# Tokens loaded in runs of two with block-diagonal K and V, a staged head and loads issued from ScalarE, in a windowed-attention and maxout feed-forward kernel

## Chip, cores and metric

One core of a Trainium2 chip. The metric is the device time of one execution in microseconds (us), median of several. A run whose time is over 1.5% above the fastest run of the same kernel is called slow; verdicts use fast runs alone, with a 95% interval, and 2% is the threshold for "faster" or "slower". Engines: TensorE (PE, its weight loads PEld), VectorE (DVE), ScalarE (ACT), GpSimd (POOL) and SyncE (SP). A "q" behind an engine's name in a profile line means its instruction stream issuing a DMA.

## The reference

Attention over 4 batches, 8 heads, 768 tokens and 64 columns per head, with a causal window of 128 and 4 sink tokens; its output, 3072 tokens of 512, goes through a three-way maxout and one more matrix.

```python
scores = scale * np.matmul(q, k.transpose(0, 1, 3, 2))
rel = pos[:, None] - pos[None, :]
keep = (pos[None, :] < n_sink) | ((rel >= 0) & (rel < window))
a = softmax(np.where(keep, scores, -1e9))          # written out in the original
x = (a @ v).transpose(0, 2, 1, 3).reshape(B * S, H * D)
h = np.maximum(np.maximum(x @ w1, x @ w2), x @ w3)  # 512 -> 768
return (h @ w_out).astype(np.float32)               # 768 -> 512
```

## The kernel before

The work is cut into 12 chunks of 256 tokens (3 per batch). For each chunk: load K, Q, V in float32 (SyncE), cast to bf16 (GpSimd), transpose K and Q (TensorE), scores, exp (ScalarE), mask (DVE), attention times V (called AV below, with a 65th column of ones that gives the softmax sum), transpose of the result, then nine groups of feed-forward matmuls (h) and two output tiles (y). The feed-forward of one chunk is interleaved with the attention of the next.

```python
def load(ci):                      # one partition per token: 256-byte runs
    for n in range(2):             # t0: the first token of half n
        for j, src in ((0, k), (1, q)):
            nc.sync.dma_start(out=qk[:, n, j], in_=src[b, :, t0:t0 + 128].rearrange("h p d -> p h d"))
    for n in range(2):
        nc.sync.dma_start(out=vr[:, n], in_=v[b, :, t0:t0 + 128].rearrange("h p d -> p h d"))

load(0)
# ... identity and masks (GpSimd) ...
for i in range(2):                 # zeros on DVE: half of each K pair is zero
    nc.vector.memset(kz[i][64:128, :, 0, :], 0.0)
    nc.vector.memset(kz[i][0:64, :, 1, :], 0.0)
    nc.vector.memset(ve[i][:, :, :, D:D + 1], 1.0)
    # ... zeros of ks ...
# ... nine weight tiles and wo, all issued by GpSimd here ...
load(1)
# ... sink rows vs_raw (SyncE), their products on GpSimd ...

def av(ci, qd, t):                 # one head per matmul: 65 columns
    # ... sink matmul ...
    for hh in range(4):
        p, h = divmod(4 * qd + hh, 2)
        # blocks: the one or two key blocks in the window
        for i, (sl, kb) in enumerate(blocks):
            nc.tensor.matmul(o[:, hh], lhsT=es[ci, p][:, h, sl], rhs=ve[b % 2][:, kb, 2 * p + h, :], ...)

cast(0, True)                      # chunk 0 on DVE and ACT
# prep(0), cast(1), load(2), all scores, AV and transposes of chunk 0,
# prep(1), cast(2), load(3), and only then the first feed-forward matmul
```

The softmax here doesn't subtract the row's maximum and nothing guards it: scores larger than these inputs give would overflow.

## Time and profile before

| | before |
|---|---|
| time, median of 3 runs | 237.43 us (236.39 to 238.04) |
| span in the profile, granted TensorE clock | 236.0 us, 1.000 |
| first score / first feed-forward matmul / first y matmul | 20.34 / 47.18 / 60.72 us |
| last matmul | 232.0 us |
| DMA packets | 84,070, of them 75,600 under 512 B |

A timeline line reads: start, duration, engine, source line, operation, output<-input, shapes, count; in brackets how long the engine had been idle and what ended it. A group line ends with busy time and mean ns, then the idle time before the group. The lines that carry the argument are in the prediction; one more is needed for comparison, the AV group:

```profile
L230 PE MATMUL o_ps<-ve,e_sb 128*128 128x65 bf16 x352 | 19.8, 197 | 5.8 <-DVE e_sb L202 4.4
```

There are 352 matmuls of 65 columns, and TensorE waited 5.8 us in all ahead of them.

### The profile page before, as it was taken

Reading aid. Unit: us, or ns where it says so; the run is one execution under the profiler, and the core shown is the slowest. Engines: PE = TensorE matmul, PEld = TensorE weight load, DVE = VectorE, ACT = ScalarE, POOL = GpSimd, SP = SyncE. Lnnn points to the kernel's source line nnn. Section 1 sums busy time; section 2 is a strip of 40 time slices with the busy share of each in tenths; the row PEclk is TensorE's granted clock in tenths of the full one; section 3 lists DMA queues with packets and bytes.
Section 4 is the critical chain, followed back from the end, with each engine's and each line's share of the span. In section 5 each row is a group of like instructions: output and inputs, shape, how many; then the busy total and the mean of one; then the engine's idle time right before and its main releaser. Section 6 shows DMA issues by size and latency. Waiting matters only on the chain.

```text
span 236.0 us, 4886 instructions
## 1 busy us (share of the span) xinstructions
PE 190.7 (81%) x1968; PEld 153.7 (65%) x1968; DVE 134.1 (57%) x307; ACT 112.9 (48%) x215; POOL 55.1 (23%) x79
## 2 busy tenths in 40 slices
PE   0025600499998999999979999999899999999993
PEld 0013400389687786887967887968768879789681
DVE  6841500247577397395685773964857739547350
ACT  2016300146465545664744547556545475574411
POOL 8840005953015005032060140330500400000000
PEclk9999999999999999999999999999999999999999
DMA  7999988990196194591881964916919720020202
GB/s 150 194 184 183 191 167 158 174 205 3 47 213 102 55 213 92 164 187 51 184 136 46 205 109 132 204 23 175 185 47 200 114 89 3 1 92 0 92 0 89
DMA packets 84070, 28.65 MB, mean 121 GB/s; under 512 B 75600, under 2 KB 80976, under 8 KB 84048
## 3 DMA queue, kind: packets, MB, share of 16 engines
q1 hardware_dynamic: 78496, 25.20, 51.0%
q0 software_dynamic: 5552, 3.15, 9.3%
q8 instruction: 15, 0.25, 0.5%
q14 instruction: 7, 0.06, 0.1%
HBM read 25.20 MB, written 6.29 MB: 133 GB/s over the span
## 4 chain that ended last, share of the span: by engine, by line
PE 57%; DVE 17%; SPq 11%; ACT 5%; DMA 4%; issue 3%; POOL 2%; POOLq 0%; ACTq 0%; DVEq 0%
PE h_ps L260 29%; PE y_ps L271 10%; SPq L64 8%; DVE h_sb L266 5%; DVE e_sb L202 5%; PE o_ps L230 4%; PE pt L163 4%; SPq L68 3%; DVE kz L170 3%; DMA v_raw<-in_v_dram 3%; PE st L191 3%; ACT e_sb L199 2%; PE xt_ps L249 2%; DVE x_sb L238 2%; ACT h_sb L264 2%
## 5 line engine op out<-in xcount | busy, mean ns | idle before, releaser
L260 PE MATMUL h_ps<-xT,w 128*128 128x256 bf16 x864 | 109.9, 274 | 0.0
L260 PEld LDWEIGHTS <-w 128*128 128x128 bf16 x864 | 81.3, 98 | 9.0
L199 ACT ACTIVATE e_sb<-st 128x512 bf16<-128x512 f32 (+1 forms) x96 | 53.8, 564 | 36.9 <-PE st L193 36.9
L202 DVE TENSOR_TENSOR e_sb<-e_sb,msk 128x1024 bf16<-128x1024 bf16 (+1 forms) x48 | 33.6, 699 | 64.4 <-ACT e_sb L199 63.9
L266 DVE TENSOR_TENSOR h_sb<-h_sb,h_ps 128x512 bf16<-128x512 bf16 x72 | 49.3, 684 | 9.6 <-PE h_ps L260 7.5
L148 POOL CAST qk_bf<-qk_raw 128x1024 bf16<-128x1024 f32 x22 | 23.8, 1086 | 103.3 <-DMA qk_raw<-in_q_dram 103.3
L163 PE MATMUL pt<-ident,qk_bf 128*128 128x128 bf16 x192 | 20.0, 236 | 33.1 <-POOL qk_bf L148 14.8
L163 PEld LDWEIGHTS <-qk_bf 128*128 128x128 bf16 x192 | 13.8, 105 | 35.1 <-POOL qk_bf L148 15.3
L271 PE MATMUL y_ps<-wo,h_sb 128*128 128x512 bf16 x144 | 35.2, 380 | 0.0
L274 ACT COPY y_sb<-y_ps 128x512 f32<-128x512 f32 x24 | 14.0, 585 | 37.1 <-PE y_ps L271 37.1
L170 DVE COPY kz<-pt 64x512 bf16<-64x512 bf16 x48 | 20.1, 418 | 17.5 <-PE pt L163 16.9
L191 PE MATMUL st<-qT,kz 128*128 128x256 bf16 x96 | 27.2, 284 | 1.9 <-ACT qT L166 1.2
L264 ACT CAST h_sb<-h_ps 128x512 bf16<-128x512 f32 x36 | 21.1, 585 | 9.9 <-PE h_ps L260 9.1
L230 PE MATMUL o_ps<-ve,e_sb 128*128 128x65 bf16 x352 | 19.8, 197 | 5.8 <-DVE e_sb L202 4.4
L230 PEld LDWEIGHTS <-e_sb 128*128 128x128 bf16 x352 | 17.2, 100 | 8.1 <-DVE e_sb L202 5.2
L166 ACT COPY qT<-pt 128x512 bf16<-128x512 bf16 x24 | 14.1, 586 | 17.0 <-PE pt L163 17.0
L193 PE MATMUL st<-qT,kz 128*128 128x128 bf16 x96 | 22.0, 229 | 0.0
L238 DVE TENSOR_TENSOR x_sb<-o_ps,rc 128x256 bf16<-128x256 f32 x48 | 20.4, 425 | 1.7
L271 PEld LDWEIGHTS <-h_sb 128*128 128x128 bf16 x144 | 12.6, 98 | 12.2 <-DVE h_sb L266 1.9
L154 POOL CAST ve<-v_raw 128x512 bf16<-128x512 f32 x22 | 14.8, 681 | 3.5 <-DMA v_raw<-in_v_dram 2.6
L250 ACT COPY xT<-xt_ps 128x512 bf16<-128x512 bf16 x24 | 13.1, 598 | 3.3 <-PE xt_ps L249 3.3
L189 PE MATMUL st<-qT,kz 128*128 128x128 bf16 x64 | 14.2, 222 | 0.0
(38 smaller groups left out, 104.6 us busy)
## 6 DMA issues: line engine op xcount, KB each, us to landing
qk_raw<-in_k_dram SPq DMA_DIRECT2D x24, 256.0 KB
qk_raw<-in_q_dram SPq DMA_DIRECT2D x24, 256.0 KB
v_raw<-in_v_dram SPq DMA_DIRECT2D x24, 256.0 KB
out_dram<-y_sb SPq DMA_DIRECT2D x24, 256.0 KB
w<-in_moe_w_dram POOLq DMA_DIRECT2D x9, 256.0 KB, 12.5
wo<-in_moe_w_out_dram POOLq DMA_DIRECT2D x2, 384.0 KB, 17.5
vs_raw<-in_v_dram SPq DMA_DIRECT2D x8, 4.0 KB
```

The lines of the kernel that those rows point to most:

```text
L148: nc.gpsimd.tensor_copy(qkb[:, n], qk[:, n].rearrange("p j h d -> p j (h d)"))
L163: nc.tensor.transpose(pt[:, p], qkb[:, n, j, p * 128:(p + 1) * 128], ident)
L170: nc.vector.tensor_copy(kz[b % 2][r, :, h, t0:t0 + 128], pt[r])
L191: nc.tensor.matmul(st[:, 1:3], lhsT=kzh[:, q0:q0 + 128], rhs=qh[:, q0:q0 + 256], start=True, stop=True)
L199: nc.scalar.activation(e[:, h, lo:], st[:, lo:], AF.Exp, scale=scale)
L202: nc.vector.tensor_mul(e[:, :, lo:], e[:, :, lo:], m)
L230: nc.tensor.matmul(o[:, hh], lhsT=es[ci, p][:, h, sl], rhs=ve[b % 2][:, kb, 2 * p + h, :], start=(c == 0 and i == 0), stop=(i == len(block ...
L238: nc.vector.tensor_mul(xs[ci, t][:, 4 * qd:4 * qd + 4], o[:, :, 0:D], rc.unsqueeze(2).to_broadcast([128, 4, D]))
L260: nc.tensor.matmul(hp[:, f], lhsT=w_sb[fp, wi][:, ds, f * 128:(f + 1) * 128], rhs=xTs[ci][:, ds, :], start=(ds == 0), stop=(ds == DS - 1))
L264: nc.scalar.copy(dst, hp)
L266: nc.vector.tensor_max(dst, dst, hp)
L271: nc.tensor.matmul(yp, lhsT=hs[ci][:, fb, t * 128:(t + 1) * 128], rhs=wo[:, fb], start=(fb == 0), stop=(fb == FB - 1))
```

## The change

It has two parts. **Layout:** a partition takes two adjacent tokens, so that a K or Q run is 512 bytes; K blocks and V blocks become block-diagonal over a pair of heads, the masks follow, and AV streams 130 columns. **Schedule:** the head of the program is staged: the sink rows come first, two groups of the loads are issued from ScalarE's stream at chosen points (so that they stay behind the arriving weights), the feed-forward of chunk 0 starts before chunk 1 is transposed, and zeros of the second batch move to GpSimd at a later point.

```diff
-        def load(ci):
-            qk = raw.tile([128, 2, 2, H, D], F32, ...)
-                    nc.sync.dma_start(out=qk[:, n, j], in_=src[b, :, t0:t0 + 128].rearrange("h p d -> p h d"))
+        def load(ci, eng):
+            qk = raw.tile([128, 2, H, 2, D], F32, ...)
+            vr = raw.tile([128, 2, NP, 2, D], F32, ...)
+            for g in range(2):
+                for j, src in ((0, k), (1, q)):
+                    eng.dma_start(out=qk[:, j, 4 * g:4 * g + 4],
+                        in_=src[b, 4 * g:4 * g + 4, t0:t0 + 256].rearrange("h (p i) d -> p h (i d)", i=2))
+            for h in range(2):
+                for n in range(2):
+                    eng.dma_start(out=vr[64 * h:64 * h + 64, n],
+                        in_=v[b, h::2, t0 + 128 * n:t0 + 128 * n + 128].rearrange("a (r i) d -> r a (i d)", i=2))
 ...
+        def zeros(i, eng):
+            eng.memset(kb_sb[i][64:128, :, :, :, :, 0:64], 0.0)
+            eng.memset(kb_sb[i][0:64, :, :, :, :, 64:128], 0.0)
+            eng.memset(vb_sb[i], 0.0)
 ...
+        zeros(0, nc.vector)
 ...
+        def sink_v_init():
 ...
+            nc.gpsimd.memset(vs, 0.0)
 ...
-                    nc.tensor.matmul(o[:, hh], lhsT=es[ci, p][:, h, sl],
-                                     rhs=ve[b % 2][:, kb, 2 * p + h, :],
+                    nc.tensor.matmul(o[:, 2 * a:2 * a + 2], lhsT=es[ci, p][:, i, sl],
+                                     rhs=vb_sb[b % 2][:, n // 2, n % 2, p, i],
 ...
+        for g in range(2):
             for j in range(2):
-                prep(0, n, j)
+                cast_qk(0, j, g, nc.vector)
+                prep(0, j, g)
+        cast_v(0)
+        run("Sa0 Sa1 Sa2", a=0)
+        load(1, nc.scalar)
+        run("Sa3 Sa4 Aa00 Sa5 Aa01 Sa6 Sa7", a=0)
+        sink_v_init()
+        sink_v(0)
         cast(1)
 ...
+        run("Fa0 Fa1 Kb0 Fa2 Qb0 Kb1 Qb1 Zb Sb0 Sb1 Sb2", a=0, b=1)
+        load(2, nc.scalar)
+        load_wo()
+        run("Fa3 Sb3 Sb4 Ab00 Fa4 Sb5 Ab01 Sb6 Fa5 Sb7 Ab10 Ab11 Tb0 Tb1", a=0, b=1)
         cast(2)
-        load(3)
+        load(3, nc.sync)
 ...
+        zeros(1, nc.gpsimd)
```

(S is a score, A an AV group, T a transpose of the result, F a feed-forward group, K and Q transposes, Z the sink scores; a and b are the chunks.)

## The prediction

> **What bounds the kernel now.** I read the page's slices first, then the groups by form, then the timeline of the head and of one steady chunk, then the chain.
>
> Slices (40 of 5.9 us each: TensorE, then DMA share):
>
> ```profile
> PE   0025600499998999999979999999899999999993
> DMA  7999988990196194591881964916919720020202
> ```
>
> TensorE is nearly empty for eight slices (47 us) while the DMA engines are full; from there on it is full to the end, and DMA has room. So there are two regimes with different limits.
>
> The head, from the timeline and the chain:
>
> ```profile
> 9.41 4.40 SPq L64 DMA_DIRECT2D qk_raw<-in_q_dram  x1
> 20.34 0.37 PE L191 MATMUL st<-qT,kz 128*128 128x256 bf16 x1 [0.67 <-ACT qT L166]
> 32.78 3.27 SPq L120 DMA_DIRECT2D vs_raw<-in_v_dram  x8
> 43.51 0.77 PEld L163 LDWEIGHTS <-qk_bf 128*128 128x128 bf16 x8 [15.05 <-POOL qk_bf L148]
> 47.18 1.92 PE L260 MATMUL h_ps<-xT,w 128*128 128x256 bf16 x8
> ```
>
> Chunk 1's loads are pushed into the SP queue while all weights stream; each issue takes 3 to 5 us. The sink rows come behind them at 32.78, and GpSimd, in order, will not cast chunk 1 before it has used the sink rows. So the first feed-forward matmul is at 47.18, although chunk 0's attention was finished at 29.35 (28.77 + 0.58, its last xT copy).
>
> The steady part: pieces of the chain, and one attention-times-V group of the timeline.
>
> ```profile
> 138.44 1.75 PE h_ps L260 x16
> 158.77 1.31 PE y_ps L271 x6
> ...
> 125.33 0.41 PE L230 MATMUL o_ps<-ve,e_sb 128*128 128x65 bf16 x8
> 125.55 0.10 PEld L220 LDWEIGHTS <-e_sink 128*128 128x128 bf16 x1
> 125.57 0.27 PE L220 MATMUL o_ps<-vs,e_sink 128*128 128x260 bf16 x1
> ```
>
> A 256-column matmul takes 1.75/16 = 109 ns, a 512-column one 1.31/6 = 218 ns, and eight 65-column AV matmuls run from 125.33 to 125.57, 30 ns each. From the starts of all matmuls in the trace I summed these costs: 178 us of necessary TensorE time; the first matmul is at 11.3 and the last at 232.0, so 43 us is idle or cold, 33 of it before the first y matmul at 60.7. The later iterations lose 0.2 to 2.0 us each, mostly before AV (DVE's mask). TensorE is **the** bound after 47 us; whatever is added to it there is paid.
>
> **What the Trainium skill says.** (1) "TensorE: Matmul & The Clock Gate", Back-to-back issue gap: warm gap is N/2.4 + 2.5 ns, which is 56 at 128, 109 at 256 and 216 at 512; the trace has 56, 109 and 216 (medians of starts). At 65 the trace has 30. (2) "DMA: Bandwidth & Descriptors", Queues, rings and completion order: each DMA engine alternates between the queues packet by packet. The packet records agree: from 10 to 24 us the SP queue moves about 490 packets of 256 B and the GpSimd queue about 494 of 512 B in each 2 us (61 and 123 GB/s), whereas the SP queue alone had 224 GB/s from 2 to 6 us. (3) The same page, Specifications: transfers need at least 512 B for line rate. No run yet shows 512 B reads here; 256 B packets took 22 ns and 2 KB packets 89 ns, so doubling the run to 512 B should cost far less than double (an estimate: 30 ns). (4) "VectorE: DVE Perf Modes", Zero memsets can be issued as uint32: a memset pays per element, whatever the type. The trace: 128x2080 bf16 in 1.79 us, 64x1536 uint32 in 1.34, both 0.87 ns per element.
>
> **The change, part by part.**
>
> *Runs of two.* A partition now holds two adjacent tokens, so Q/K/V packets are 512 B and half as many: 36,900 instead of 73,700. In the steady part DMA was not the limit (GpSimd's cast waits, 103 us in total, hold nobody up there), so this is worth nothing after 47 us. In the head it is: load 0 has 3,072 packets; at 30 ns on 16 engines about 6 us, so it lands near 9 us. Before, its last part was cast at 17.92 us.
>
> *Block-diagonal K.* Scores keep their number and columns: 8 x (128+256+128). Transposes, exps, masks and DVE copies keep count and size too (the instruction order shows 3,938 TensorE rows on both sides). Zero.
>
> *Block-diagonal V.* AV keeps 352 matmuls, but each streams both heads' columns, 130 instead of 65. By the formula that the other sizes obey, 130/2.4 + 2.5 = 57 ns instead of 30: 352 x 27 = **+9.5 us** of TensorE, all but 24 of the matmuls in or near the full part. I let 1 us of it be absorbed by waits for DVE: +8.5.
>
> *GpSimd and DVE.* Casts per chunk go from 2 x 1.09 + 2 x 0.68 = 3.5 us to about 4 x 0.65 + 2 x 1.1 = 4.8 us, out of 16: hidden. DVE's zeros at the start: 2 x 1.34 + 6,240 x 0.87 ns = 5.4 + small ones, ending near 10.6 us, as before (10.7). So earlier data doesn't start DVE's first cast earlier. The second batch's zeros go to GpSimd, some 13 us at its 1.02 ns per element (512 in 0.52 us); they lie between the casts of chunks 2 and 3, and TensorE needs the latter near 67 us, about when they are done: 0 to 2 us.
>
> *The staged head.* A walk with durations from the trace. DVE casts, K copies and sink copies in a chain with transposes: 10.6 to about 16.6, first score there (20.34 before, because ACT's qT copy stood behind the V cast, now on GpSimd). Exps at 0.53 us each; after the third, ACT issues load 1's eight DMAs. One issue took SP 0.41 us even for 4 KB (3.27/8), so **ACT is held 3.3 us at least**, up to 5 if the queue fills behind the weights. Remaining exps, AV, transposes: about 5.8 us. First feed-forward matmul at 18.2 + 4.1 + 0.5 + 5.8 = 28.6, against 47.18. Three of its groups and chunk 1's transposes and scores take to about 37.5; then load 2's issues hold ACT again for 3.3 to 4 us, of which TensorE has work for 1.5. Chunk 1's attention with groups 3 to 5 then takes 6 us, so TensorE is full from about 47.5. By then 15.1 us of its work are done, so 32.4 us are lost; 1.5 more for the less regular schedule of chunk 2: **34**.
>
> Sum: before, start and loss up to 60.7 were 44.0 (11.3 + 32.7); now 34. Work 178 becomes 187.5. Later losses were 10.0; with one iteration fewer and the absorbed microsecond, 7.5. Last matmul at 34 + 187.5 + 7.5 = 229, against 232.0. Last copy, store and end as before, 4 us: span 233, and the measured time was 1.4 above the span: 234.4.
>
> **The rivals.**
> (a) *The ACT issues are cheap or fall beside other work.* For it: they are a deliberate gate, so that load 1 stays behind the weights. Against: 0.41 us per issue on SP. It would give back up to 5 us: 229.
> (b) *The head collapses further*, since TensorE gets warm earlier and load 1 lands early: 226. Against: DVE's memsets fix the start at 10.6, and scores to xT took 9 us before.
> (c) *DMA back-pressure.* Load 1 alternates with 1 KB weight packets (96 ns each before), ACT is held for more than 5 us, twice. For it: SP's 3 to 5 us per issue before. It gives 237 to 239.
> (d) *AV's added columns hide.* They would if weight loads set the 30 ns, but the rule gives 57 ns for the stream itself, above any of them. I give it little; it would mean 226.
>
> **Range and chances.** The sum says 234.4. I lean to (a) a little, since gate and order look tuned on the chip, and put the time at 232, range 226 to 237.5. The 2% line is 232.7, just above: faster 0.54, within 2% 0.44, slower 0.02.
>
> **What will show it.** Starts of AV matmuls 57 ns apart, and AV's busy time up accordingly; 512 B packets at about 30 ns, 3,072 per load; DVE's first cast near 10.6; a gap of 3 to 5 us between the third and fourth exp of chunk 0, with ACT's DMA issues in it, and another in chunk 1; the first feed-forward matmul at 27 to 30; the PE row at 9 from the eighth or ninth slice. The prediction fails if AV is not 57 ns, if ACT's issues cost much less or more than 3.3 us, or if chunk 3's late zeros or a slower GpSimd cast open a new hole between 55 and 75 us.

## The result and the profile after

The changed kernel takes **250.68 us** (median of four fast runs, 250.38 to 252.25) against 237.74 (236.39 to 238.24). The ratio is 1.0567, 95% interval 1.0503 to 1.0631: slower. (A ratio here is the mean time of one kernel's fast runs over that of the other's in the same rounds, so not quite the ratio of the medians.) The result is correct.

From the starts of all matmuls I made the same sum as in the prediction. "Lost" is time in which TensorE had no matmul to do or ran one at a lower rate. (Twelve of the 144 y records are missing in the later traces; 12 x 0.216 us is put back as work.)

| us | before | predicted | after |
|---|---|---|---|
| start and time lost up to the first y matmul | 44.0 | 34 | **47.0** |
| needed TensorE work | 178 | 187.5 | 187.5 |
| lost later | 10.0 | 7.5 | 10.3 |
| last matmul | 232.0 | 229 | 244.7 |

The work is what was predicted. The head, which should have gained 10 us, lost 3. The slices of the page (6.2 us each) show where: TensorE's share rises early, then there is a hole in the eighth slice, and the clock dips in and behind it.

```profile
PE   0024487067999698999989999999899999999994
PEclk9999999758999999999999999999999999999999
DMA  6998996710001986183490671914806720020102
```

The timeline of the first half of the head:

```profile
5.48 5.26 DVE L93 MEMSET vb<- 128x6240 bf16 x1 [1.25 <-issue]
...
11.68 0.47 DVE L161 CAST qk_bf<-qk_raw 128x512 bf16<-128x512 f32 x1
...
13.68 1.82 POOL L146 MEMSET vs<- 128x2080 bf16 x1
13.76 1.80 DVE L202 COPY ks<-kb 128x4 bf16<-128x4 bf16 x4
...
20.93 0.43 ACTq L66 DMA_DIRECT2D qk_raw<-in_k_dram  x1
...
23.07 2.68 ACTq L71 DMA_DIRECT2D v_raw<-in_v_dram  x4
...
25.80 0.87 ACT L226 ACTIVATE e_sb<-st 128x384 bf16<-128x384 f32 x2 [4.39 <-DMA qk_raw<-in_k_dram]
...
26.93 0.40 PE L257 MATMUL o_ps<-vb,e_sb 128*128 128x130 bf16 x2 [4.78 <-DVE e_sb L228]
...
34.09 3.19 PE L288 MATMUL h_ps<-xT,w 128*128 128x256 bf16 x16 [0.67 <-ACT xT L277]
```

DVE clears V until 10.74 and casts first at 11.68. Four tiny copies take 1.80 us while GpSimd clears `vs`. ScalarE issues load 1 from 20.93 to 25.75 and starts no exp in that time; AV waits 4.78 us for it. The first feed-forward matmul is at 34.09, 13 us earlier than before. Its 16 matmuls take 3.19 us, against 16 x 0.109 = 1.75 at full rate.

The second hold:

```profile
43.97 0.52 ACTq L66 DMA_DIRECT2D qk_raw<-in_q_dram  x1
45.48 4.54 ACTq L71 DMA_DIRECT2D v_raw<-in_v_dram  x4
45.55 0.60 POOL L161 CAST qk_bf<-qk_raw 128x512 bf16<-128x512 f32 x1 [12.38 <-DMA qk_raw<-in_k_dram]
46.34 0.61 POOL L161 CAST qk_bf<-qk_raw 128x512 bf16<-128x512 f32 x1 [0.18 <-DMA qk_raw<-in_q_dram]
48.17 0.61 POOL L161 CAST qk_bf<-qk_raw 128x512 bf16<-128x512 f32 x1 [1.22 <-DMA qk_raw<-in_k_dram]
49.44 0.61 POOL L161 CAST qk_bf<-qk_raw 128x512 bf16<-128x512 f32 x1 [0.66 <-DMA qk_raw<-in_q_dram]
50.05 0.58 ACT L292 CAST h_sb<-h_ps 128x512 bf16<-128x512 f32 x1 [7.09 <-POOL qk_bf L161]
...
52.07 0.62 PE L257 MATMUL o_ps<-vb,e_sb 128*128 128x130 bf16 x4 [8.08 <-DVE e_sb L228]
52.48 1.91 PE L288 MATMUL h_ps<-xT,w 128*128 128x256 bf16 x8
...
61.29 6.28 PE L288 MATMUL h_ps<-xT,w 128*128 128x256 bf16 x56
```

ScalarE's next work comes at 50.05; since 42.43 (the start of its first issue of load 2) it had only issued DMAs: 7.6 us. Narrower windows give the starts of the four V issues: 45.48, 46.3, 48.14 and 49.41. GpSimd's casts, which wait for the K and Q transfers of the same load, start at 45.55, 46.34, 48.17 and 49.44. The semaphore records have these four transfers landed at 45.40, 46.29, 48.12 and 49.39. So each V issue went out at the moment when one K or Q transfer of its own load had landed. AV then waited 8.08 us; the eight matmuls behind it took 1.91 us, where eight later ones take 1.04, and TensorE is dense from 61.29, not from the predicted 47.5.

The AV group, and two lines of the steady part:

```profile
L257 PE MATMUL o_ps<-vb,e_sb 128*128 128x130 bf16 x352 | 31.4, 230 | 19.2 <-DVE e_sb L228 19.0
```

```profile
76.37 0.62 PE L257 MATMUL o_ps<-vb,e_sb 128*128 128x130 bf16 x8
76.83 0.22 PE L216 MATMUL st<-qT,kb 128*128 128x128 bf16 x1
```

Eight AV matmuls occupy 76.37 to 76.83, 57 ns each, as predicted; the waits in front of the group grew from 5.8 to 19.2 us, which are the two holes.

### The profile page after: what moved, and what is told of

It reads as the page before. It is cut to its first block, busy times and chain, and to the rows that moved or that the text cites. A ratio compares the mean times of both kernels' runs of the same rounds, so it can differ in the third digit from the quotient of the medians.

```text
span 248.7 us, 4928 instructions
## 1 busy us (share of the span) xinstructions
PE 202.2 (81%) x1956; PEld 164.4 (66%) x1968; DVE 139.5 (56%) x306; ACT 115.1 (46%) x213; POOL 84.7 (34%) x109
## 2 busy tenths in 40 slices
DMA packets 46006, 28.66 MB, mean 115 GB/s; under 512 B 2208, under 2 KB 42912, under 8 KB 45984
## 4 chain that ended last, share of the span: by engine, by line
PE 60%; DVE 21%; ACT 8%; issue 5%; ACTq 2%; DMA 2%; POOL 0%; DVEq 0%
PE h_ps L288 28%; PE y_ps L299 11%; PE o_ps L257 8%; DVE e_sb L228 5%; ACT e_sb L226 5%; DVE kb L194 4%; DVE h_sb L294 4%; PE pt L186 4%; PE st L218 3%; DMA qk_raw<-in_q_dram 2%; DVE vb L93 2%; PE xt_ps L276 2%; DVE ks L202 2%; ACT qT L189 2%; DVE x_sb L265 2%
## 5 line engine op out<-in xcount | busy, mean ns | idle before, releaser
L288 PEld LDWEIGHTS <-w 128*128 128x128 bf16 x864 | 82.5, 99 | 10.9 <-issue 1.0
L161 POOL CAST qk_bf<-qk_raw 128x512 bf16<-128x512 f32 x44 | 27.8, 636 | 106.4 <-DMA qk_raw<-in_k_dram 86.4
L257 PE MATMUL o_ps<-vb,e_sb 128*128 128x130 bf16 x352 | 31.4, 230 | 19.2 <-DVE e_sb L228 19.0
L257 PEld LDWEIGHTS <-e_sb 128*128 128x128 bf16 x352 | 25.1, 102 | 23.2 <-DVE e_sb L228 21.9
L299 PE MATMUL y_ps<-wo,h_sb 128*128 128x512 bf16 x132 | 32.7, 379 | 0.6
L170 POOL CAST vb<-v_raw 64x1024 bf16<-64x1024 f32 x24 | 27.0, 1125 | 6.2 <-DMA v_raw<-in_v_dram 5.3
L218 PE MATMUL st<-qT,kb 128*128 128x256 bf16 x96 | 27.1, 286 | 0.7 <-ACT e_sb L226 0.7
L189 ACT COPY qT<-pt 128x512 bf16<-128x512 bf16 x24 | 17.5, 735 | 20.8 <-PE pt L186 20.8
L220 PE MATMUL st<-qT,kb 128*128 128x128 bf16 x96 | 22.0, 229 | 0.0
L194 DVE COPY kb<-pt 64x512 bf16<-64x512 bf16 x48 | 20.1, 419 | 3.0 <-PE pt L186 2.5
L277 ACT COPY xT<-xt_ps 128x512 bf16<-128x512 bf16 x24 | 13.2, 595 | 8.5 <-PE xt_ps L276 8.5
L216 PE MATMUL st<-qT,kb 128*128 128x128 bf16 x64 | 14.2, 221 | 0.4 <-ACT e_sink L238 0.3
```

The costliest lines, as they stand in the source:

```text
L161: eng.tensor_copy(bfs[ci][:, j, g].rearrange("p i (h d) -> p h i d", d=D), qk[:, j, 4 * g:4 * g + 4])
L170: nc.gpsimd.tensor_copy(vb_sb[b % 2][hp, c, :, :, :, h, 0:D].rearrange("p n a i d -> p (n a i) d"), vr[hp].rearrange("p n a i d -> p (n a ...
L194: nc.vector.tensor_copy(kb[hp, c, :, 2 * g:2 * g + 2, :, 64 * h:64 * h + 64] .rearrange("p i a n r -> p i (a n) r"), pt[hp].rearrange("p i ...
L218: nc.tensor.matmul(st[:, 1:3], lhsT=kb[:, c, i, p, 0], rhs=qh[:, q0:q0 + 256], start=True, stop=True)
L257: nc.tensor.matmul(o[:, 2 * a:2 * a + 2], lhsT=es[ci, p][:, i, sl], rhs=vb_sb[b % 2][:, n // 2, n % 2, p, i], start=(c == 0 and x == 0), s ...
L288: nc.tensor.matmul(hp[:, f], lhsT=w_sb[wi, 2 * fp + f][:, ds], rhs=xTs[ci][:, ds, :], start=(ds == 0), stop=(ds == DS - 1))
```

## The experiments

They ran on three chips (e1 to e4, e5 to e8, e9 to e12), each time beside the kernel before, whose medians there were 237.36, 236.7 and 236.9 us. So a comparison of runs from two of these groups leans on chips that agree within 0.7 us. The table has the medians of the fast runs, of four where nothing else is said; "hf" is the first feed-forward matmul in the profile.

| run | what it is | us | ratio to before | hf |
|---|---|---|---|---|
| before | | 237.74 | 1 | 47.18 |
| changed | | 250.68 | 1.0567 | 34.09 |
| e1 | before, AV with 130 columns | 241.53 | 1.0194 (1.015 to 1.0237) | |
| e2 | changed, loads 1 and 2 from SyncE | 236.76 | 0.9989 (0.9948 to 1.0031) | 29.94 |
| e3 | changed, load 2 alone from SyncE | 248.67 | 1.0468 | 42.12 |
| e4 | old layout, staged head, SyncE | 226.88 (3 of 4 fast) | 0.9631 (0.9575 to 0.9686) | 24.01 |
| e5 | new layout, old order | 237.21 | 1.0033 (0.9972 to 1.0095) | 40.02 |
| e6 | old layout, staged head, ScalarE | 241.61 (the one fast run; the slow ones 246.66 to 246.83) | none | |
| e7 | e2, V zeros on GpSimd | 234.64 | 0.9908 (0.9864 to 0.9952) | 26.83 |
| e8 | e4, weights behind load 0 | 227.0 (3 of 4 fast) | 0.9588 (0.9513 to 0.9664) | 19.69 (slow run) |
| e9 | e2, zeros chunk by chunk | 230.61 and 231.28 (2 of 4 fast; the slow ones 234.08, 234.23) | none | 21.18 |
| e10 | changed, load 3 from ScalarE too | 252.19 (3 of 4 fast) | 1.0618 | |
| e11 | changed, sink zeros later | 249.20 | 1.0491 (1.0437 to 1.0544) | 32.84 |
| e12 | e2 with old V and AV | **226.19** | 0.9535 (0.9482 to 0.9587) | 20.33 |

The theory after the result: two costs sit side by side, ScalarE held by the loads that it issues, and the 130-column AV. The rivals: the layout's other costs (copies, transposes, late zeros) or the staged order itself.

### e1: the wider AV alone

```diff
-   nc.tensor.matmul(o[:, hh], ..., rhs=ve[b % 2][:, kb, 2 * p + h, :], ...)
+   nc.tensor.matmul(o[:, hh - h:hh - h + 2], ..., rhs=ve[b % 2][:, kb, 2 * p:2 * p + 2, :], ...)
```

The values are wrong: both heads' V are added under each head's weights; the cost is the changed kernel's.

> The kernel before with one thing changed: each of its 352 attention-times-V matmuls streams the V columns of both heads of the pair (130) instead of one head's (65). The values are wrong on purpose (the second head's V is added in), only the time counts. Theory A (the added columns are paid in full, since TensorE is the bound after the head): starts of AV matmuls 57 ns apart instead of 30, total 8 to 9.5 us longer, 246 to 247 us. Rival (the columns hide behind waits for DVE or behind weight loads): under 2 us, 237 to 240 us.

It took 241.53, 4 us more, between the two expectations; the verdict against before is "unclear". The first y is where it was (60.54 against 60.72). From there to the last matmul the needed work grew by 8.1 us, but the lost time shrank from 10.0 to 6.2: TensorE had been waiting for DVE's masks in just those places, and the longer AV fills some of the wait. So the work is real and 3.8 us of it is absorbed, where the prediction allowed 1.

### e2: loads 1 and 2 from SyncE

```diff
-        load(1, nc.scalar)
+        load(1, nc.sync)
-        load(2, nc.scalar)
+        load(2, nc.sync)
```

> The changed kernel with loads 1 and 2 issued from SyncE's queue instead of ScalarE's; nothing else. Theory A (ScalarE is held 4.8 us by load 1's eight issues and 7.6 us by load 2's, the last four of which wait for the first four to land; TensorE then also runs at a low clock): both holes before AV vanish, the first feed-forward matmul comes at 28 to 30 us instead of 34.1, total 10 to 14 us shorter, 237 to 241 us. Rival B (TensorE waits for chunk 2's and chunk 1's data anyway, so the holes move to the transposes): 246 us or more. Rival C (the early loads take bandwidth from the weights and delay the feed-forward): first feed-forward matmul not before 33 us, 244 us or more.

236.76: 13.9 us come back by changing which engine issues two loads. The slices have no hole in the eighth place any more, and the profile's granted clock is 1.000:

```profile
PE   0025787798987899999899999998999999999993
```

Start and lost time up to the first y are 33.8 us instead of 47.0; the needed work is 187.4 and the later loss 9.2. The holds of 4.8 and 7.6 us, 12.4 together, are nearly all of the 13.2 us between the two heads. SyncE itself is held longer (load 1's issues run from 10.02 to 22.91, beside the arriving weights), but no computation stands behind it.

### e3: load 2 alone from SyncE

```diff
-        load(2, nc.scalar)
+        load(2, nc.sync)
```

> The changed kernel with only load 2 issued from SyncE's queue; load 1 still holds ScalarE. Theory A: the hole of 8.25 us before chunk 1's first AV and the half clock behind it go, 8 to 10 us shorter, 241 to 243 us; the hole of 5 us in chunk 0 stays. If the semaphore waits of the last four issues are not what holds ScalarE, the hole stays and the time is 249 or more.

A miss: 248.67, only 2 us better. Taking away the second hold made the first longer:

```profile
27.24 6.65 ACTq L71 DMA_DIRECT2D v_raw<-in_v_dram  x4
...
33.94 0.87 ACT L226 ACTIVATE e_sb<-st 128x384 bf16<-128x384 f32 x2 [11.74 <-DMA v_raw<-in_v_dram]
...
42.12 1.23 PE L288 MATMUL h_ps<-xT,w 128*128 128x256 bf16 x5 [0.67 <-ACT xT L277]
```

ScalarE issues the K and Q of load 1 from 21.71 to 23.81, but its V issues start only at 27.24, and it is back at 33.94. The records of the issues in the trace say why. The DMAs of SyncE and ScalarE share eight completion semaphores, 101 to 108, in this program, and a DMA that is to use one again waits first for its earlier user. In the changed kernel load 1's eight issues carry eight different numbers. Load 2's K and Q carry 101, 103, 105 and 107, and its V the same four once more, because load 3 on SyncE has 102, 104, 106 and 108: so each V issue waits for the landing of one K or Q transfer, which is the pairing of times at 45 to 50 us above. In e3 the same sharing has moved to load 1, whose V reuses the four numbers of its own K and Q, with load 2 on SyncE in the other four. The clock of this profile was 1.000 with nearly the same total as the changed kernel, so the clock dip after the second hole is not the main cause either.

### e10: load 3 from ScalarE as well

```diff
-        load(3, nc.sync)
+        load(3, nc.scalar)
```

If SyncE's load 3 makes load 2's issues wait, taking load 3 off SyncE must shorten the second hold, though it adds a third.

> The changed kernel with load 3 also issued from ScalarE (after chunk 1's transposes), so that the eight completion semaphores go to load 2 in order and none of its DMAs waits for another of the same load. Theory (the extra 2.8 us of load 2's hold over load 1's are the wait for its own first four DMAs): load 2 holds ScalarE 4.5 to 5 us instead of 7.6, the hole before chunk 1's first AV is 5 to 6 us instead of 8.25; load 3 adds a hold of about 5 us in which TensorE has feed-forward work. Rival (the queue itself swallows no faster): hold of 7 us or more as before. The total may go either way, 246 to 252.

252.19, and the second hold is 4.8 us (43.09 to 47.85) instead of 7.6, the wait before AV 5.12 us instead of 8.08:

```profile
45.24 2.61 ACTq L71 DMA_DIRECT2D v_raw<-in_v_dram  x4
...
49.76 0.61 PE L257 MATMUL o_ps<-vb,e_sb 128*128 128x130 bf16 x4 [5.12 <-DVE e_sb L228]
...
65.84 4.31 PE L288 MATMUL h_ps<-xT,w 128*128 128x256 bf16 x24 [3.00 <-ACT h_sb L292]
```

Load 2's eight issues carry eight different numbers here, and the four V issues take 2.61 us, not 4.54. A third hold opens a new hole of 3 us at 65.84. The rival reading, that load 3's traffic on the SyncE queue had slowed load 2 down, falls with the packets of the changed kernel between 42 and 54 us (queue: packets, MB, share of 16 engines; q10 is ScalarE's, q1 SyncE's):

```profile
q10 hardware_dynamic: 3200, 1.57, 47.5%
q1 hardware_dynamic: 60, 0.03, 0.8%
```

Load 2 had the engines to itself.

### e4, e5 and e6: layout and schedule apart

e4 has the old layout (natural tokens, zero-padded K per head, 65-column AV) under the staged order, with all loads from SyncE. e6 is e4 with loads 1 and 2 from ScalarE. e5 has the new layout under the old order and the old loads.

```diff
 # e4, against e2
-   qk = raw.tile([128, 2, H, 2, D], ...); vr = raw.tile([128, 2, NP, 2, D], ...)
-   kb_sb, vb_sb, block-diagonal; masks by parity; AV 130 columns
+   qk = raw.tile([128, 2, 2, H, D], ...); vr = raw.tile([128, 2, H, D], ...)
+   kz, ve, masks, prep, score and av of the kernel before
 # e6, against e4
+   load(1, nc.scalar) ... load(2, nc.scalar)
 # e5, against the kernel before: its load, kb_sb, vb_sb, masks, prep, score, av;
 #   zeros of both batches on DVE; order and loads as before
```

> The staged head of the change, loads from SyncE's queue, but tokens, K, V and masks as in the kernel before (256-byte runs, K zero-padded per head, AV with 65 columns). Theory A (the layout costs 9 us of AV and the larger runs give little): 10 us or more below the version with loads from SyncE and the new layout, 223 to 230 us, the fastest so far. Rival (512-byte runs are what makes the staged head work, since 256-byte loads cross the weights at 61 GB/s): loads 1 lands only near 30 us, first feed-forward groups wait, 234 us or more.

> The change's layout alone (runs of two tokens, block-diagonal K and V) in the order of work, of loads and of weights of the kernel before, all loads from SyncE, both batches' zeros on VectorE before its first cast. Theory: the steady part pays about 4 us for AV, as the kernel with 130 columns did; in the head each turn of the SyncE queue beside the weights moves 512 B instead of 256, so chunk 1 and the sink rows land earlier and the first feed-forward matmul comes near 40 instead of 47 us. Sum 233 to 238 us. Rival (the head is not limited by the load queue, or 17 us of zeros on VectorE take its place): first feed-forward matmul at 46 or later, 241 us or more.

> The change's order and staging alone, with loads 1 and 2 from ScalarE as in the change, but the layout of the kernel before (256-byte runs, six DMAs per load, so no DMA of one load waits for another of the same load). Theory A (ScalarE is held as long as its DMA queue takes to swallow a load): the hold by load 1, 1,024 descriptors per DMA beside the weights, is 8 us or more, and the total 10 to 20 us above the same kernel with loads from SyncE (227.8): 238 to 248. Rival (only the waits for semaphores of the same load hold ScalarE): holds of under 4 us, total 232 or less.

e4 is **faster than both kernels**, 226.88. Its last matmul is 10.4 us before that of e2. The sums of the two traces split this: 9.4 us less work, 4.9 us less loss up to the first y (28.9 against 33.8), and 3.8 us more loss later (13.0 against 9.2). That is e1's absorption again, found in another pair. e4 is not free of waits: chunk 0's V, in 256-byte packets while the weights arrive, comes late.

```profile
18.07 0.61 POOL L159 CAST ve<-v_raw 128x512 bf16<-128x512 f32 x1 [5.11 <-DMA v_raw<-in_v_dram]
...
24.01 1.23 PE L270 MATMUL h_ps<-xT,w 128*128 128x256 bf16 x5 [0.67 <-ACT xT L259]
```

e5 moves nothing: 237.21. Its last matmul is at 231.0 although the first feed-forward matmul came 7 us earlier (40.02): an earlier start and the wider AV seem to cancel. The head starts late, since DVE clears both batches first:

```profile
16.39 5.26 DVE L88 MEMSET vb<- 128x6240 bf16 x1 [1.25 <-issue]
...
24.76 1.36 DVE L157 CAST qk_bf<-qk_raw 128x512 bf16<-128x512 f32 x4
```

e6 is worse than before in each of its runs; three were slow; its one fast run, 241.61, is 14.7 us above the fast median of e4. Its profile is of a slow run. There the six issues of load 1, with 256-byte runs, hold ScalarE from 12.53 to 27.25, also 14.7 us:

```profile
20.55 4.35 ACTq L66 DMA_DIRECT2D qk_raw<-in_q_dram  x1
...
27.30 0.87 ACT L208 ACTIVATE e_sb<-st 128x384 bf16<-128x384 f32 x2 [14.29 <-DMA qk_raw<-in_q_dram]
```

One single issue took 4.35 us. It is tempting to blame the short runs (the changed kernel's first hold is 4.8 us), but no run shows that. Load 1 starts 8 us earlier in e6, and packets of the weights arrive until about 24 us; in the changed kernel they end near 22, just after load 1 begins. The second and third issue also waited about 3.7 us in all, until sink rows that had used their semaphores landed (16.07 and 17.01). With 512-byte runs beside the weights, SyncE was held 12.9 us by load 1 (e2). And e6's own load 2, with 256-byte runs and no weights around, held ScalarE 5.4 us (43.51 to 48.91), less than the changed kernel's 7.6. (That load's two V issues also went out when its own K and Q landed, at 46.79 and 48.02; the expectation had ruled this out.) With loads from SyncE the old layout is better by 10 us.

### e11: the sink zeros later

```diff
-        sink_v_init()
-        sink_v(0)
         cast(1)
+        sink_v_init()
+        sink_v(0)
```

> The changed kernel with GpSimd's sink-row set-up (a 1.8 us memset and small ones, 13.1 to 17.2 us) moved behind chunk 1's casts. Theory (GpSimd's memset blocks VectorE's SBUF-to-SBUF copies for its whole length): the four tiny copies of chunk 0's sink keys take 0.4 us instead of 1.8, first score 1.3 to 1.8 us earlier than 19.03, total 1 to 2 us shorter. Rival: they stay at 1.8 us.

249.20, 1.5 us less (all four runs, 248.02 to 249.90, lie below the changed kernel's 250.38 to 252.25, on another chip). The copies that took 1.80 us beside GpSimd's memset now take 0.39:

```profile
13.77 0.39 DVE L202 COPY ks<-kb 128x4 bf16<-128x4 bf16 x4
```

and everything behind moves up by about as much: ScalarE's first issue from 20.93 to 19.58, the first feed-forward matmul from 34.09 to 32.84.

### e7 and e9: the zeros of V

V was never cleared before. In the changed kernel its 128x6240 zeros (5.26 us) stand on DVE ahead of chunk 0's first cast. Both runs are e2 with these zeros elsewhere; e9 splits K's zeros in the same way.

```diff
 # e7: V's zeros of batch 0 on GpSimd, behind the weights' issues
-            eng.memset(vb_sb[i], 0.0)
+            nc.gpsimd.memset(vb_sb[i], 0.0)
 # e9: only chunk 0's zeros first on DVE; the rest on GpSimd after chunk 0's casts
-        zeros(0, nc.vector)
+        zeros(0, nc.vector, slice(0, 1))
+        zeros(0, nc.gpsimd, slice(1, CPB))      # further down, before sink_v_init()
```

> The changed kernel with loads 1 and 2 from SyncE, and V's zeros and ones (5.3 us on VectorE before its first cast) moved to GpSimd behind the weights' issue. Theory (V's zeros stand on the path of the head): VectorE's first cast at 5.5 to 7 us instead of 11.7, total 4 to 6 us below the 236.8 of the version with loads from SyncE, 231 to 233. Rival (GpSimd's long memset blocks VectorE's copies, as its memset of the sink rows seems to block four tiny copies for 1.8 us in the changed kernel): first score at 17 us or later, 235 or more.

> The changed kernel with loads 1 and 2 from SyncE, and batch 0's zeros split: VectorE clears only what chunk 0 reads (a third, about 3 us with gaps instead of 9.5), GpSimd clears the rest after it has cast chunk 0's V. Theory (V's zeros are what the layout costs in the head): VectorE's first cast at 5.5 to 6.5 us, no new hole before chunk 0's AV, first feed-forward matmul at 23.5 to 25 instead of 29.9, total 230 to 232 against 236.8; what is left over the natural layout (227.8) is AV. Rival (chunk 1's data then sets the pace): first feed-forward early, but total 234 or more.

e7 gains 2 us over e2, less than expected. Chunk 0's K and Q start at once (its first transposes at 4.86), but V's cast has to wait for GpSimd's memset, and AV stands 6.1 us behind it:

```profile
11.31 5.30 POOL L96 MEMSET vb<- 128x6240 bf16 x1
...
19.58 0.59 PE L260 MATMUL o_ps<-vb,e_sb 128*128 128x130 bf16 x4 [6.10 <-POOL vb L173]
```

e9 clears a third first and keeps both engines free:

```profile
2.48 1.79 DVE L93 MEMSET vb<- 128x2080 bf16 x1 [0.38 <-issue]
...
4.93 0.41 DVE L162 CAST qk_bf<-qk_raw 128x512 bf16<-128x512 f32 x1
...
21.18 3.15 PE L289 MATMUL h_ps<-xT,w 128*128 128x256 bf16 x14 [0.67 <-ACT xT L278]
```

The first cast is at 4.93 and the first feed-forward matmul at 21.18, against 29.94 in e2. The two fast runs, 231.28 and 230.61, are some 6 us below e2. So the zeros, V's and K's together, cost about that much, and the layout's remaining distance from e4 is about 4 us. Against e4, e9 has 9.4 us more work, 2.4 us less loss up to the first y (26.6) and about 1.5 us less loss later: in this pair the waits absorb less than the 3.8 us of the other two.

### e8 and e12: towards a better version

e8 holds the weights back until chunk 0's casts are issued, in e4. e12 keeps the runs of two for K and Q alone, with K zero-padded per head as before, V loaded in the matching order of rows, and AV with 65 columns.

```diff
 # e8, against e4
+        cast_v(0)
+        # weight DMAs here instead of at the top
 # e12, against e2
-   kb_sb = [128, CPB, 2, NP, 2, 128] block-diagonal; vb_sb; masks [128, 2, 4, 128]
+   kb_sb = [128, CPB, 2, NP, 2, 2, 64]  # one half zero per head; rows even, then odd
+   eng.dma_start(out=vr[64 * i:64 * i + 64, n], in_=v[...].rearrange("h (r i) d -> i r h d", i=2)[i])
+   ve, av as before; masks [128, 4, 128] by row parity
```

> The natural layout with the staged head and loads from SyncE (227.8 us), the weights' DMAs issued only when chunk 0's V has landed and is cast. Theory (the hole of 4.2 us before chunk 0's AV is V crossing the weights in 256-byte packets): that hole goes, first feed-forward matmul at 20 to 21 us instead of 24.0, total 223 to 225.5. Rival (the weights, later by 5 us and beside load 1, then hold the feed-forward): 227 or more.

> A version made of what paid: staged head, loads from SyncE, K and Q in 512-byte runs, K zero-padded per head with its keys in the order of the runs, V in 256-byte rows laid in that same order, so that AV streams 65 columns and V needs no zeros. Expected 223 to 226 us, below the 227.8 of the natural layout, because chunk 0's V and chunk 1's K land earlier; if the head is not set by the loads' packets, 227 to 229.

e8 brings nothing over e4 (227.0 and 226.88): the first feed-forward matmul comes 4.3 us earlier, at 19.69, but now load 1 crosses the weights, and chunk 1's transposes wait 5.4 us for GpSimd's cast, up to 29.45. (The profile of e8 is of a slow run; only the order of events is read from it.) e12 has the lowest median, **226.19**, just above what was expected; it is correct, 4.7% faster than before (0.9482 to 0.9587) and 10% faster than the changed kernel. It is within the error of e4 and e8, so K and Q in 512-byte runs show no gain over the old layout here.

## Why the prediction was wrong

**The step that failed is the price of issuing from ScalarE.** The prediction put it at 3.3 us at least, "up to 5 if the queue fills behind the weights", and used 4.1 for the first hold and a net 2 for the second. Measured: 4.8 and 7.6 us, and the second opened a hole of 8 us in TensorE, not of 2. Without these holds (e2) the head loses 33.8 us; with them, 47.0. So they cost 13.2 us where 6.1 (4.1 and 2) was put down. These 7.1 us are the largest part of the 13 us by which the head was worse than predicted; the other 5.9 are in the rest of the walk, which e2 has too (33.8, where 34 - 6.1 = 27.9 was put down). The first hold was of the right size (its issues are 0.43 to 0.69 us each, against the 0.41 us taken from SyncE). The second was mis-sized because an issue was thought to cost only its own time or a full queue; here it also waited for the landing of earlier transfers, through shared completion semaphores (e3, e10). The overlap of 1.5 us was right: TensorE had work until 43.98. But behind the hold a cast, an exp and a mask, 2.0 us (50.05 to 52.07), still stood before AV, and these were not counted: in e10 a hold of 4.8 us, without the waits for its own load, still made a hole of 5.1. Rival (c), ScalarE held for more than 5 us, named the right mechanism, with another cause, and gave it 237 to 239, far too little. The lean towards rival (a) went the wrong way.

**The walk to the first score** came out at 19.03, not 16.6. DVE's zeros ended 1.1 us late (first cast 11.68, not 10.6), since the trace shows a gap of 1.25 us in front of the large memset that was not in the sum, and GpSimd's memset cost 1.4 us of DVE time (e11). The Trainium skill's "SBUF — State Buffer", section "SBUF: two separate sides", says that a GpSimd instruction and a DVE instruction in a two-port mode lock their shared port pair for the whole instruction; 1.80 against 0.39 us agrees with it, if these copies ran in such a mode, which no run shows.

**From the end of the hold to the first feed-forward matmul** it took 8.3 us (25.75 to 34.09), where 5.8 was put down. The trace shows slower masks there (0.81 and 0.96 us, against 0.56) beside GpSimd's casts, and slower matmuls; no run separates the two.

**The zeros as neutral.** The prediction said that DVE's zeros end "as before" and so change nothing. That was true of the comparison with before and hid the point: a staged head could have started 6 us earlier (e9, e4).

**AV was right in mechanism, and its absorption mis-sized.** The added 9.5 us of work and the 57 ns are there. Of the 8 us that fall after the first y, the waits absorbed 3.8, not 1 (e1; e2 against e4), or about 1.5 (e9 against e4). This error went the other way. In the changed kernel the later loss stayed at 10.3, not 7.5: some 4.6 us of it fall between 79.6 and 100.9, in the transition to the regular schedule, for which 1.5 had been allowed.

**What was right:** K and Q packets of 512 B, half as many (46,006 packets in all, from 84,070); their mean duration in the SyncE queue was 35 ns, median 27, where 30 was estimated from 22 ns for 256 B. The layout of the head was right too: first feed-forward matmul well before 47, and a gap between the third and fourth exp with the DMA issues in it. GpSimd's late zeros took 12 us and opened no hole. One cost was overlooked and stayed hidden: ScalarE's qT copies, which now write every second element, took 735 ns instead of 586.

The whole: predicted sum 234.4, stated 232.0. The trace adds 13 us to the head and 2.8 to the later loss. 229 + 13 + 2.8 is 244.8, the last matmul that was measured (244.7). Two small readings were off without weight: in the profiled run before, time less span is 237.76 - 236.0 = 1.8 us, not 1.4, and 1.79 us for 2080 elements is 0.86 ns each.

What stays open is what the clock dip after the second hole costs by itself, why the walk from the first hold was 2.5 us longer, and whether the length of the runs changes a hold.

## What to carry to other kernels

Here a DMA issued from ScalarE kept it from computing until the issue had gone through (0.4 to 0.7 us each, up to 4.35 beside the weights), and some issues waited for the landing of an earlier transfer; a gate made in this way belongs on a stream with nothing behind it. A layout that needs zeros should clear at first only what the first tile reads, for in this kernel these memsets stood ahead of the whole pipeline (some 6 us). When work is added to the busiest engine, look first at what it waits for in that very place: here 3.8 of some 8 us of added work went into waits that were there already in two pairs of runs, and about 1.5 us in a third.

## What the Trainium skill lacked or had wrong

- "DMA: Bandwidth & Descriptors", section "Issuing engines are not separate DMA queues", says that issuing from several engines only saves the sequencer's time, "usually small relative to the DMA itself". It does not say what that time costs when the issuing engine also computes, and I found no page with its size: the issues held ScalarE for 4.8, 7.6 and (e6, a slow run) 14.7 us, and moving two loads to SyncE was worth 13.9 us of 250.7. Nor did I find the case of an issue that waits for the earlier user of its own completion semaphore: with four semaphores used twice, eight issues held ScalarE 7.6 us, with eight different ones 4.8 (the changed kernel's load 1, and load 2 in e10).
- "TensorE: Matmul & The Clock Gate", section "Back-to-back issue gap", gives sustained spacings of about 81 ns at 128 columns and 131 ns at 512 in real kernels, and calls the simple formula one for isolated matmuls. The traces here have 56 and 216 ns in a full stream, 57 at 130 columns and 30 at 65: the formula held and the sustained figures did not.
- "SBUF — State Buffer", section "Door 1: The DMA port swizzle", says that accesses can stride for free up to 8 bf16 elements. Here a ScalarE copy of 128x512 bf16 from PSUM took 735 ns when writing every second element of SBUF and 586 ns when writing contiguously. I found no page with a time for such a copy.
